# First layer from its second block on: two steps' first products, then two steps' second products

## The chip, the cores and the metric

The kernel runs on one core of one Trainium2 chip. The metric is the device time of one execution in microseconds (us); lower is better. The engines are named as in the profile: PE is the matrix engine, with PEld for its weight loads and PEq for its sequencer; DVE is the vector engine, ACT the scalar engine, POOL the GpSimd engine, and SP the engine that issues nearly all DMAs (its queue is SPq).

## What is computed

```python
x = attn_out.transpose(0, 2, 1, 3).reshape(B * S, H * D)    # 3072 tokens x 320
# attn_out: a gated recurrent attention (mLSTM) over q, k, v, i_gate, f_gate, o_gate
# B, H, S, D = 4, 8, 768, 40

# first layer: w_in 320 x 2048, w_out 2048 x 320
h = x @ w_in
x = (h - np.tanh(h)) @ w_out

# second layer: weights of the same shapes
h = x @ w_in
g = np.where(h >= 1, h, np.where(h <= -1, 0.0, (h + 1) ** 2 / 4))
out = g @ w_out
```

## The kernel before

The 3072 tokens are cut into six blocks of four chunks of 128 tokens (512 tokens to a block). The attention is done in 24 jobs, one for each chunk, in the form of matrix products: t_s holds the scores, d the decay factors (a scan over a broadcast row fb, L460) and then scores times decays (L493), t_n the numerators, t_x the transposed result, t_c the state. A block of the first layer needs the attention of its four chunks.

Each layer works on a block in 16 **steps**, one for each 128 of the 2048 hidden columns. Step f of a block has two parts on PE. The **first products** (`step`, L650) fill one PSUM bank h with 128 hidden columns x 512 tokens: eight matmuls of 512 columns, because x and the weights are each split in a high and a low part. The **second products** (`second`, L702) multiply the result with w_out and add into four banks a, one for each chunk: twelve matmuls of 320 columns. Between the two, in the first layer, four instructions run in a chain: tanh on ACT (L668), h minus tanh on DVE (L669, in the bank itself), the high part gh on ACT (L681), and the low part gl on DVE (L682). When gl is written, the bank h is free again. The second products of a step are issued two steps after its first products (`LAG = 2`). There are two banks for h, and three buffers each of gh and gl (`LAG + 1`).

The second layer has the same shape, but its steps go in groups of four (`GS`): four half-height matmuls that serve all four steps (`rows64`, L629), then the 28 other first products of the four steps, then 48 second products of four earlier steps. Its four h banks are the two of the first layer and two that the attention used.

The order is not written out by hand. Each instruction is given to a planner (`Plan`) with an engine, an estimated duration and a priority; the planner runs through time and gives each engine, among the operations that can start within 150 ns of the first, the one with the lowest priority number. What comes out is a fixed order for each engine. The priority of step i (counted through all blocks and both layers) is about i; that of its elementwise work is i - 3.5 and i - 3; that of the second products issued with it is i + 0.5. The priorities of the attention jobs of block k + 1 are spread over the 16 steps of block k, so attention runs between the steps of the first layer's blocks 0 to 4; in its last block there is none. In the same stretch DVE and ACT also convert the weights (64-bit to 32-bit, L320 to L333), and those of the second layer are stored and loaded again.

Of the kernel before, what the change touches and what calls it, by code (L numbers as in the profile page):

```python
# [56 lines left out]
GS = 4  # L57
# [18 lines left out]
class Plan:  # L76
# [20 lines left out]
    def op(self, eng, ns, prio, fn, r=(), w=(), out=None, lock=False):  # L97
        o = Op()
        o.eng, o.ns, o.prio, o.fn, o.seq, o.out = eng, ns, prio, fn, len(self.ops), out
        o.allocs, o.preds, o.succs = [], set(), []  # L100
        o.bufs, o.fill, o.lock = [], 0, lock
        key = lambda x: x if isinstance(x, tuple) else (x, None)

        for x in map(key, r):
            if x in self.last:
                o.preds.add(self.last[x])
            self.read.setdefault(x, []).append(o)
        for x in map(key, w):
            if x in self.last:
                o.preds.add(self.last[x])  # L110
            o.preds.update(self.read.pop(x, ()))
            self.last[x] = o
        o.preds.discard(o)
        for b in {key(x)[0] for x in (*r, *w)}:
            if isinstance(b, Buf):
                b.users.append(o)
                o.bufs.append(b)
        if any(b.place[0].startswith("late_") for b in o.bufs):
            o.preds.add(self.gate)
        self.ops.append(o)  # L120
        return o
# [110 lines left out]
def mlstm_moe_moe(ctx: ExitStack, tc: tile.TileContext, ig, fg, qk, qk3, q3, nat, w1, w2, cst, out):  # L232
# [63 lines left out]
    def load64(layer, f, prio):  # L296

        if layer == 0 and f in RAW:
            t = wbuf(RAW[f], [128, 8 * WC], U8, "w64")
        else:  # L300
            t = abuf("w64", [128, 8 * WC], U8, 2)
        raw_w[layer, f] = t
        load(prio, lambda: t[:, 0:8 * WC - 3], lambda: (w1, w2)[layer][f].bitcast(U8)[:, 3:8 * WC],
             704, w=[t], rows=5629)
# [23 lines left out]
    def split_w(layer, f, prio):  # L328
        u, a = w32.pop((layer, f))
        w = wt[layer, f] = wbuf(f, [128, 2 * WC], F32R, f"w{f}")  # L330
        op("ACT", act(WC), prio, lambda: nc.scalar.copy(w[:, 0:WC], a()), [u], [(w, 0)])

        vec(prio, WC, lambda e: e.tensor_tensor(  # L333
            out=w[:, WC:2 * WC], in0=a(), in1=w[:, 0:WC].bitcast(F32), op=ALU.subtract), [u, (w, 0)], [(w, 1)])
# [283 lines left out]
    def rows64(k, f, prio):  # L618

        n = BLK[k] * L  # L620
        x, y = x1[1, k], xd[k]
        for j in range(GS):
            hb[f + j] = bank(HTAGS[j], "h")

        def go():
            for j in range(GS):
                r = slice(j % 2 * 64, j % 2 * 64 + 64)
                a = x[r, 4, :n] if j % 2 == 0 else y[r, :n]
                nc.tensor.matmul(hb_[j][:, :n], wt[1, f + j][r, WC + 256:WC + 384], a, start=True, stop=False)  # L629

        hb_ = [hb[f + j] for j in range(GS)]
        op("PE", 200 + GS // 2 * pe(n), prio, go, [*((wt[1, f + j], 1) for j in range(GS)), *xkeys(1, k, 2), y], hb_)

    def step(layer, k, f, prio):
        n = BLK[k] * L
        p = None if layer else bank("h", "h")
        if wide(layer, k, f):
            w, x = wf[f], xf[0]
            for i in range(3):
                op("PE", 2 * pe(n, 128, 2), prio, lambda i=i: nc.tensor.matmul(  # L640
                    p[:, :n], w[:, i * 128:(i + 1) * 128].bitcast(F32), x[:, i, :n], start=(i == 0), stop=(i == 2)),
                   [w, *((x, m) for m in range(BLK[0]))], [p])
            return activate(layer, n, p, prio, True)
        w, x = wt[layer, f], x1[layer, k]
        seq = [(0, 0), (128, 1), (0, 2), (128, 3), (256, 4), (WC, 0), (WC + 128, 1), (WC + 256, 4)]
        if layer:
            p = hb.pop(f)
            seq.pop()
        for i, (c, s) in enumerate(seq):
            op("PE", pe(n), prio, lambda i=i, c=c, s=s: nc.tensor.matmul(  # L650
                p[:, :n], w[:, c:c + 128], x[:, s, :n], start=(i == 0 and not layer), stop=(i == len(seq) - 1)),
               [(w, int(c >= WC)), *xkeys(layer, k, s // 2)], [p])
        return activate(layer, n, p, prio, False)
# [32 lines left out]
    def second(layer, k, f, g, prio):  # L686
        n = BLK[k] * L
        w = wf[f] if wide(layer, k, f) else wt[layer, f]
        gh, gl = g
        first, last = f == 0, f == NF - 1  # L690
        if first:
            acc[k] = [bank(f"a{i}", "a") for i in range(BLK[k])]
        for s in range(BLK[k]):
            A = acc[k][s]
            r = slice(s * L, (s + 1) * L)
            if gl is None:
                seq = [(gh, 384, None)]
            else:
                seq = [(gh, 384, 0), (gh, 384 + WC, 1), (gl, 384, 0)]
            for i, (a, c, key) in enumerate(seq):  # L700
                dt = F32R if gl is not None else F32
                op("PE", pe(DM) if gl is not None else 2 * pe(DM, 128, 2), prio, lambda A=A, r=r, a=a, c=c, i=i, dt=dt: nc.tensor.matmul(  # L702
                    A[:, 0:DM], a[:, r], w[:, c:c + DM].bitcast(dt), start=first and i == 0, stop=last and i == len(seq) - 1),
                   [(w, key), a], [A])
# [65 lines left out]
    def background(f, prio):  # L770
        conv64(1, f, prio)
        u, a = w32.pop((1, f))
        load(prio + 0.5, lambda: w2_d[f], a, 352, [u], [("w2_d", f)], rows=2816)

    def reload(f, prio):
        t = lbuf("w2", [128, WC], F32, 5)
        load(prio, lambda: t.t, lambda: w2_d[f], 352, [("w2_d", f)], [t], rows=2816)
        w32[1, f] = t, lambda: t.t
# [28 lines left out]
    def jobs(k):  # L807
        for i, (a, _) in enumerate(GROUPS):
            if i and a * B == BLK0[k]:
                gates(i, GATES[i])  # L810
                decays(i, DECAYS[i])
        for n in range(BLK0[k], BLK0[k] + BLK[k]):
            if k == 0:
                job(n, lambda s: JOB0 + JOBD * n + JOBS * s, LOAD[n])
            else:
                st = NF * (k - 1) + NF * (n - BLK0[k]) / BLK[k] - AHEAD
                job(n, lambda s: st + s, st - LOADS)
# [12 lines left out]
    for i, (layer, k, f) in enumerate(steps):  # L830
        if layer == 0 and f == 0 and 0 < k < NB - 1:
            jobs(k + 1)
        if i == NF:
            for h in range(NF):
                load64(1, h, NF + 4 * h - 8)
                background(h, NF + 1 + 4 * h)
        if i == n1 - NF:

            def turn():
                att.close()  # L840
                late["p"] = ctx.enter_context(tc.tile_pool(name="late", bufs=1, reuse_waits="tile"))
            P.gate = op("X", 0, i, turn)
            P.gate.preds.update(o for o in P.ops if any(b.place[0] in att_tags for b in o.bufs))
            for h in range(NF):
                reload(h, i + max(0, h - 2))
            for h in range(NF):
                split_w(1, h, i + h + LAG + 1)
            layer2_x(0, i)
        if layer == 1 and f == 0 and k + 1 < NB:
            layer2_x(k + 1, i)  # L850
        u = i - f % GS if layer else i
        if layer and f % GS == 0:
            rows64(k, f, i)
        g[i] = step(layer, k, f, u + 0.01 * (i - u))
        if i == 0:
            P.end_warm = next(o for o in reversed(P.ops) if o.eng == "PE")

            op("PE", 0, i, lambda: None, [], [spare]).preds.add(P.end_warm)
        if i >= LAG:
            p = u + 0.5 + 0.01 * (i - u)  # L860
            second(*steps[i - LAG], g.pop(i - LAG), p)
            if steps[i - LAG][2] == NF - 1:
                evac(*steps[i - LAG][:2], p + 0.005)
# [69 lines left out]
```

## Time and profile before

| what | us |
|---|---|
| median of 3 runs | 816.76 |
| the 3 runs | 816.03 to 818.01 |
| profiled execution | 814.9 |
| its span (first to last instruction) | 813.1 |
| PE busy in the span | 803.5 |

The span is what the trace shows; 1.8 us of the profiled execution lie outside it. The profiled execution is 1.9 us below the median of the runs. The first layer's blocks 1 to 5 lie at about 105 to 475 us of the span, and the second layer behind them. A matmul's row in the trace begins when it is issued and lasts until its modelled end, so rows of neighbouring matmuls overlap; the distance from start to start is what one costs.

### The profile page before, as it was taken

The numbers are of one execution on the slowest core, as the hardware profiler recorded it, in microseconds if no ns is written. First come the engines' busy times: TensorE is split into PE (matmuls) and PEld (weight loads), VectorE is DVE, ScalarE is ACT, GpSimd is POOL, SyncE is SP. The second block draws the span as 40 slices with busy tenths as digits, with TensorE's granted clock in tenths as the row PEclk, the third lists the DMA queues.
The fourth block names the chain that finished last, engine by engine and source line by source line (L and its number), as shares of the span: only waits on it lengthen the run. The fifth ranks groups of instructions, "written<-read, shape, count | busy, mean of one in ns | idle before, by whom it ended". The sixth has DMA issues, their size and how long they took to land.

```text
span 813.1 us, 15218 instructions
## 1 busy us (share of the span) xinstructions
PE 803.5 (99%) x6030; PEld 692.8 (85%) x6034; DVE 570.3 (70%) x922; ACT 429.6 (53%) x810; POOL 147.5 (18%) x147
## 2 busy tenths in 40 slices
PE   9999999999999999999999999999999999999998
PEld 6656888888898888888899888898888889898887
DVE  6899989878888998887456684554646555564644
ACT  4866775675586677544455553443525435342432
POOL 3242122314234335332110200200200201000000
PEclk9999999999999999999999999999999999999999
DMA  8888356686758768771543120100100000000000
GB/s 263 311 261 271 101 194 175 165 260 160 202 164 243 206 188 230 214 178 45 150 116 100 53 72 1 40 33 1 40 33 1 32 1 1 33 1 1 34 1 32
DMA packets 62980, 93.66 MB, mean 115 GB/s; under 512 B 4701, under 2 KB 45501, under 8 KB 62909
## 3 DMA queue, kind: packets, MB, share of 16 engines
q1 hardware_dynamic: 62860, 92.66, 39.2%
q8 instruction: 47, 0.77, 0.4%
q14 instruction: 25, 0.20, 0.1%
q10 hardware_dynamic: 48, 0.03, 0.0%
HBM read 78.88 MB, written 13.80 MB: 114 GB/s over the span
## 4 chain that ended last, share of the span: by engine, by line
PE 90%; DMA 3%; DVE 2%; issue 1%; ACT 1%; SPq 1%; POOL 0%; POOLq 0%; ACTq 0%
PE a L702 40%; PE h L650 37%; PE h L640 3%; PE t_n L529 2%; PE h L629 2%; PE t_n L520 1%; PE t_s L473 1%; PE t_c L558 1%; PE t_s L489 1%; DMA nat<-in_nat_dram 1%; PE t_x L551 1%; DMA w_d<-w 1%; SPq L286 1%; DMA gb<-gr_d 1%; DMA fr_d<-fr 0%
## 5 line engine op out<-in xcount | busy, mean ns | idle before, releaser
L650 PE MATMUL h<-x,w 128*128 128x512 f32 x1376 | 350.1, 397 | 0.1
L702 PE MATMUL a<-w,gh 128*128 128x320 f32 x1472 | 329.3, 310 | 0.0
L650 PEld LDWEIGHTS h<-x,w 128*128 128x128 f32 x1376 | 249.5, 188 | 52.2 <-issue 6.8
L702 PEld LDWEIGHTS a<-w,gh 128*128 128x128 f32 x1472 | 250.0, 188 | 11.0 <-ACT ob L725 1.8
L702 PE MATMUL a<-w,gl 128*128 128x320 f32 x736 | 227.5, 310 | 0.0
L673 DVE TENSOR_SCALAR g<-h 128x512 f32<-128x512 f32 x96 | 63.7, 684 | 114.1 <-PE h L650 114.1
L675 ACT ACTIVATE g<-g,half 128x512 f32<-128x512 f32 x96 | 67.0, 721 | 135.5 <-DVE g L673 135.0
L702 PEld LDWEIGHTS a<-w,gl 128*128 128x128 f32 x736 | 138.2, 188 | 0.3
L669 DVE TENSOR_TENSOR h<-h,g 128x512 f32<-128x512 f32 x88 | 61.2, 695 | 44.0 <-ACT g L668 43.9
L677 DVE TENSOR_TENSOR g<-h,g 128x512 f32<-128x512 f32 x96 | 64.7, 692 | 27.1 <-ACT g L675 26.1
L681 ACT CAST gh<-g 128x512 fp32r<-128x512 f32 x96 | 59.5, 622 | 44.3 <-DVE g L677 43.6
L668 ACT ACTIVATE g<-h 128x512 f32<-128x512 f32 x88 | 52.5, 597 | 53.4 <-PE h L650 52.8
L766 POOL TENSOR_TENSOR x<-xl,x 128x512 fp32r<-128x512 f32 x18 | 25.0, 1420 | 278.1 <-ACT x L757 278.1
L681 ACT CAST gh<-h 128x512 fp32r<-128x512 f32 x88 | 51.4, 585 | 45.3 <-DVE h L669 45.0
L682 DVE TENSOR_TENSOR gl<-h,gh 128x512 fp32r<-128x512 f32 x88 | 60.1, 683 | 19.1 <-ACT gh L681 17.3
L682 DVE TENSOR_TENSOR gl<-g,gh 128x512 fp32r<-128x512 f32 x96 | 62.1, 687 | 4.0 <-ACT gh L681 1.2
L460 DVE TENSOR_TENSOR_SCAN d<-fb,scan_id 128x512 f32<-128x512 f32 x40 | 54.6, 1376 | 1.9 <-DMA fb<-fr_d 1.8
L486 POOL TENSOR_TENSOR xf<-qkraw,xf 120x1024 fp32r<-120x1024 f32 x12 | 32.6, 2713 | 38.1 <-ACT xf L484 34.4
L484 ACT ACTIVATE xf<-qkraw,cs 120x512 fp32r<-120x512 f32 x48 | 32.5, 716 | 6.1 <-PE t_s L489 6.0
L493 DVE TENSOR_TENSOR d<-t_s,d 128x512 f32<-128x512 f32 x48 | 32.0, 681 | 4.4 <-PE t_s L489 2.9
L539 POOL TENSOR_TENSOR nat<-nat,dn 128x320 f32<-128x320 f32 x24 | 21.0, 874 | 70.3 <-DVE dn L538 70.3
L500 POOL TENSOR_TENSOR nat<-nat,isT 128x328 f32<-128x328 f32 x24 | 22.6, 952 | 57.9 <-DMA nat<-in_nat_dram 37.2
(103 smaller groups left out, 765.2 us busy)
## 6 DMA issues: line engine op xcount, KB each, us to landing
w<-in_w_dram SPq DMA_DIRECT2D x32, 703.6 KB
nat<-in_nat_dram SPq DMA_DIRECT2D x24, 484.0 KB
qkraw<-in_qk_dram SPq DMA_DIRECT2D x24, 480.0 KB
fb<-fr_d SPq DMA_DIRECT2D x40, 256.0 KB
w_d<-w SPq DMA_DIRECT2D x16, 352.0 KB
w<-w_d SPq DMA_DIRECT2D x16, 352.0 KB
qkraw<-in_qk_dram SPq DMA_DIRECT2D x24, 160.0 KB
xr_d<-xo SPq DMA_DIRECT2D x24, 160.0 KB
```

The source lines that it names most:

```text
L460: op("DVE", dve(1024), p, lambda o=dk[u][0], i=f[u][0]: nc.vector.tensor_tensor_scan(out=o(), data0=i(), data1=scan_id, initial=0.0, op0=A ...
L484: op("ACT", act(512, 1), at(u - 1), lambda raw=raw, t=t, z=z, cols=cols: nc.scalar.activation(t[:, cols], raw[:, cols], AF.Copy, scale=cs[ ...
L486: vec(at(u - 1), 1024, lambda e, raw=raw, t=t: e.tensor_tensor(out=t.t, in0=raw.t, in1=t.t.bitcast(F32), op=ALU.subtract), [raw, t], [t], ...
L650: op("PE", pe(n), prio, lambda i=i, c=c, s=s: nc.tensor.matmul(p[:, :n], w[:, c:c + 128], x[:, s, :n], start=(i == 0 and not layer), stop= ...
L668: op("ACT", act(n), prio + 0.5 - FFN, lambda: nc.scalar.activation(t[:, :n], p[:, :n], AF.Tanh), [p], [t])
L669: op("DVE", dve(n), prio + 0.5 - FFN, lambda: nc.vector.tensor_tensor(out=p[:, :n], in0=p[:, :n], in1=t[:, :n], op=ALU.subtract), [p, t], [p])
L673: op("DVE", dve(n), prio + 0.5 - FFN, lambda: nc.vector.tensor_scalar(t[:, :n], p[:, :n], -1.0, 1.0, op0=ALU.max, op1=ALU.min), [p], [t])
L675: op("ACT", act(n, 1), prio + 0.5 - FFN, lambda: nc.scalar.activation(t[:, :n], t[:, :n], AF.Square, bias=half[:, 0:1], scale=0.5), [t, "h ...
L677: op("DVE", dve(n), prio + 0.5 - FFN, lambda: nc.vector.tensor_tensor(out=t[:, :n], in0=p[:, :n], in1=t[:, :n], op=ALU.max), [p, t], [t])
L681: op("ACT", act(n), prio + 1 - FFN, lambda: nc.scalar.copy(gh[:, :n], y[:, :n]), [y], [gh])
L682: op("DVE", dve(n), prio + 1 - FFN, lambda: nc.vector.tensor_tensor(out=gl[:, :n], in0=y[:, :n], in1=gh[:, :n].bitcast(F32), op=ALU.subtra ...
L702: op("PE", pe(DM) if gl is not None else 2 * pe(DM, 128, 2), prio, lambda A=A, r=r, a=a, c=c, i=i, dt=dt: nc.tensor.matmul(A[:, 0:DM], a[: ...
```

## The change

The priority of a step in the first layer was its number i. From the second block on (k > 0) it is now that of the even step of its pair, plus 0.01 for the odd one; the same goes for its second products and for its elementwise work. The planner does the rest, for all engines.

```diff
@@ -848,7 +848,7 @@
             layer2_x(0, i)
         if layer == 1 and f == 0 and k + 1 < NB:
             layer2_x(k + 1, i)
-        u = i - f % GS if layer else i
+        u = i - f % (GS if layer else 2 if k > 0 else 1)
         if layer and f % GS == 0:
             rows64(k, f, i)
         g[i] = step(layer, k, f, u + 0.01 * (i - u))
```

The instructions are the same ones in the same number. What follows is the order on three places; the numbers behind w_ tell the weight tiles of the steps apart.

First, PE in the last block of the first layer, where no attention runs. Before, from the first products of step 8 (w_752) to those of step 9 (w_916):

```order
L650 MATMUL h<-x_4521,w_752 128x512 x8
L702 MATMUL a<-w_1853,gh 128x320 x2
L702 MATMUL a<-w_1853,gl 128x320
L702 MATMUL a<-w_1853,gh 128x320 x2
L702 MATMUL a<-w_1853,gl 128x320
L702 MATMUL a<-w_1853,gh 128x320 x2
L702 MATMUL a<-w_1853,gl 128x320
L702 MATMUL a<-w_1853,gh 128x320 x2
L702 MATMUL a<-w_1853,gl 128x320
L650 MATMUL h<-x_4521,w_916 128x512 x8
```

Of the change, from the same first products on:

```order
L650 MATMUL h<-x_4523,w_752 128x512 x8
L650 MATMUL h<-x_4523,w_916 128x512 x8
L702 MATMUL a<-w_1849,gh 128x320 x2
L702 MATMUL a<-w_1849,gl 128x320
L702 MATMUL a<-w_1849,gh 128x320 x2
L702 MATMUL a<-w_1849,gl 128x320
L702 MATMUL a<-w_1849,gh 128x320 x2
L702 MATMUL a<-w_1849,gl 128x320
L702 MATMUL a<-w_1849,gh 128x320 x2
L702 MATMUL a<-w_1849,gl 128x320
L702 MATMUL a<-w_1874,gh 128x320 x2
```

The two steps' first products now stand together, and so do two steps' second products. Over the whole program PE goes from second products straight to first products (a row L702, then a row L650) 87 times before and 40 times now.

Second, the second block, around its step 7 (weight tile w_1897 before, w_1874 in the change, whose low part L333 is made just then; fb, C, x, d and t_s belong to the attention). DVE before, from gl of step 6 to gl of step 7:

```order
L682 TENSOR_TENSOR gl<-h,gh 128x512
L602 TENSOR_TENSOR x_1700<-t_x,x_1700 128x2x128
L606 TENSOR_TENSOR x_1700<-t_x,x_1700 64x128
L357 COPY carry<-mg 32x1
L669 TENSOR_TENSOR h<-h,g 128x512
L493 TENSOR_TENSOR d<-t_s,d 128x512
L682 TENSOR_TENSOR gl<-h,gh 128x512
```

DVE of the change, from gl of step 6 to gl of step 7:

```order
L682 TENSOR_TENSOR gl<-h,gh 128x512
L324 SCALAR_TENSOR_TENSOR w_1306<-w_1251,w_1306 128x704
L333 TENSOR_TENSOR w_1874<-wf,w_1874 128x704
L575 SCALAR_TENSOR_TENSOR C<-C,gb,t_c 80x82
L602 TENSOR_TENSOR x_1698<-t_x,x_1698 128x2x128
L606 TENSOR_TENSOR x_1698<-t_x,x_1698 64x128
L460 SCALAR_TENSOR_TENSOR d<-fb,scan_id 128x512
L669 TENSOR_TENSOR h<-h,g 128x512
L493 TENSOR_TENSOR d<-t_s,d 128x512
L682 TENSOR_TENSOR gl<-h,gh 128x512
```

PE of the change at that place, from the low-part products of step 7 to the first products of step 9 (w_916), which use the same bank:

```order
L650 MATMUL h<-x_806,w_752 128x512 x2
L650 MATMUL h<-x_806,w_1874 128x512 x3
L650 MATMUL h<-x_806,w_752 128x512
L473 MATMUL t_s<-qkraw 128x128 x8
L650 MATMUL h<-x_806,w_752 128x512 x5
L520 MATMUL t_n<-C,q_1762 128x123 x2
L520 MATMUL t_n<-C,q_1762 128x82
L650 MATMUL h<-x_806,w_916 128x512 x7
```

Three more long DVE instructions stand ahead of step 7's chain, and between the end of step 7's first products and those of step 9 there are now no second products.

Third, PE where the second layer begins (L629 is `rows64`; w_1213 and w_1266 are the first layer's last two steps). Before, from the first rows64 on:

```order
L629 MATMUL h<-x_5167,w_5292 128x512
L629 MATMUL h<-xd,w_5325 128x512
L629 MATMUL h<-x_5167,w_5358 128x512
L629 MATMUL h<-xd,w_5391 128x512
L650 MATMUL h<-x_5167,w_5292 128x512 x7
L650 MATMUL h<-x_5167,w_5325 128x512 x7
L650 MATMUL h<-x_5167,w_5358 128x512 x7
L650 MATMUL h<-x_5167,w_5391 128x512 x7
L702 MATMUL a<-w_1266,gh 128x320 x2
L702 MATMUL a<-w_1266,gl 128x320
```

Of the change, from one row ahead of the first rows64 on:

```order
L702 MATMUL a<-w_1213,gh 128x320
L629 MATMUL h<-x_5184,w_5310 128x512
L629 MATMUL h<-xd,w_5324 128x512
L629 MATMUL h<-x_5184,w_5376 128x512
L629 MATMUL h<-xd,w_5390 128x512
L650 MATMUL h<-x_5184,w_5310 128x512 x7
L650 MATMUL h<-x_5184,w_5324 128x512 x7
L650 MATMUL h<-x_5184,w_5376 128x512 x7
L650 MATMUL h<-x_5184,w_5390 128x512 x7
L702 MATMUL a<-w_1213,gh 128x320
L702 MATMUL a<-w_1213,gl 128x320
```

Before, the 12 second products of w_1266 were all that stood between the 28 first products and the next rows64; now 11 of w_1213 stand there as well.

## Rows read from the trace of the kernel before

**Rows 1.** The page's first part: busy us (share of the span), instructions.

```profile
PE 803.5 (99%) x6030; PEld 692.8 (85%) x6034; DVE 570.3 (70%) x922; ACT 429.6 (53%) x810; POOL 147.5 (18%) x147
```

**Rows 2.** Busy time by stretch: stretch, its us, then each engine's busy us.

```profile
85.00:480.00 395.00, 392.43 (x3321) 346.76 (x3321) 314.32 (x520) 241.66 (x479) 104.97 (x99) 1.00 0.57 161
...
398.00:462.00 64.00, 64.00 (x357) 57.95 (x356) 37.59 (x53) 33.23 (x55) 3.79 (x3) 1.00 0.43 121
```

**Rows 3.** The chain that ended last: start, us, what; one step of the last block.

```profile
441.21 1.84 PE h L650 x8
443.05 1.75 PE a L702 x12
```

**Rows 4.** PE in order of time: one matmul, then 15 inside a long run.

```profile
441.05 0.39 PE L650 MATMUL h<-x,w 128*128 128x512 f32 x1
...
608.79 3.56 PE L650 MATMUL h<-x,w 128*128 128x512 f32 x15
```

**Rows 5.** In order of time, one step's chain in the last block.

```profile
442.88 0.45 PE L702 MATMUL a<-w,gh 128*128 128x320 f32 x2
...
443.42 0.60 ACT L668 ACTIVATE g<-h 128x512 f32<-128x512 f32 x1 [1.24 <-PE h L650]
...
445.40 0.69 DVE L682 TENSOR_TENSOR gl<-h,gh 128x512 fp32r<-128x512 f32 x1 [0.66 <-ACT gh L681]
```

**Rows 6.** In order of time on PE: waits in the first layer, in brackets.

```profile
144.94 0.52 PE L551 MATMUL t_x<-cs,x 128*128 128x128 f32 x3 [0.38 <-DVE x L546]
...
185.42 0.76 PE L520 MATMUL t_n<-C,q 120*128 120x123 f32 x5 [0.68 <-POOL q L510]
...
331.78 0.21 PE L370 MATMUL t_i<-cs,ig 32*128 32x32 f32 x1 [0.77 <-DVE x L606]
```

**Rows 7.** In order of time, DVE and PE where the second layer begins.

```profile
464.46 0.50 PE L629 MATMUL h<-x,w 64*128 64x512 f32 x1
...
465.12 6.66 PE L650 MATMUL h<-x,w 128*128 128x512 f32 x28
...
473.05 1.35 DVE L677 TENSOR_TENSOR g<-h,g 128x512 f32<-128x512 f32 x2 [0.19 <-ACT g L675]
...
473.47 0.50 PE L629 MATMUL h<-x,w 64*128 64x512 f32 x1
...
474.88 2.11 PE L650 MATMUL h<-x,w 128*128 128x512 f32 x8
```

**Rows 8.** DVE in order of time in the second block.

```profile
132.47 0.42 DVE L602 TENSOR_TENSOR x<-t_x,x 128x256 fp32r<-128x256 f32 x1
132.91 0.28 DVE L606 TENSOR_TENSOR x<-t_x,x 64x128 fp32r<-64x128 f32 x1
133.22 1.23 DVE L460 TENSOR_TENSOR_SCAN d<-fb,scan_id 128x512 f32<-128x512 f32 x1
134.36 0.67 DVE L669 TENSOR_TENSOR h<-h,g 128x512 f32<-128x512 f32 x1
134.95 0.69 DVE L493 TENSOR_TENSOR d<-t_s,d 128x512 f32<-128x512 f32 x1
...
137.29 0.85 DVE L333 TENSOR_TENSOR w<-wf,w 128x704 fp32r<-128x704 f32 x1
138.07 0.87 DVE L322 TENSOR_TENSOR w<-w,cvb 128x704 int32<-128x704 f32 x1
```

**Rows 9.** POOL in order of time in the second block.

```profile
142.42 0.75 POOL L510 TENSOR_TENSOR q<-q,gb 120x256 f32<-120x256 f32 x1 [2.87 <-PE a L702]
...
143.53 0.73 POOL L539 TENSOR_TENSOR nat<-nat,dn 128x320 f32<-128x320 f32 x1
```

**Rows 10.** SP's queue and DVE: broadcasts issued, and the scan that waited.

```profile
175.20 1.29 SPq L286 DMA_DIRECT2D fb<-fr_d  x2
...
182.91 1.22 DVE L460 TENSOR_TENSOR_SCAN d<-fb,scan_id 128x512 f32<-128x512 f32 x1 [1.22 <-DMA fb<-fr_d]
```

**Rows 11.** PE in order of time: t_s of a job.

```profile
133.76 1.16 PE L473 MATMUL t_s<-qkraw 40*128 40x128 f32 x16
```

## The prediction

> **What bounds the kernel now.** I read the page's busy times first. PE is busy for 99% of the span, DVE for 70%, ACT for 53% [rows 1]. So PE sets the end, and the change can act in two ways only: through what PE's instructions cost in another order, and through the moments at which PE stands still. The instructions are the same, so nothing else can be saved.
>
> How much standing still is there? The busy time by stretch gives 392.43 us of PE in the 395 us from 85 to 480, in which the changed steps lie: 2.57 us idle, and none in the 64 us of the last block, where no attention runs [rows 2]. A wait is longer than its idle time by the modelled end of the matmul ahead of it, some 0.15 us (the last matmul's 0.39 us against the 0.23 us that one costs), so all waits together are some 4 us. The order of time on PE shows the longest: a t_x that waits for x, a t_n that waits for q, a t_i that waits until the t_x before it is read [rows 6]. All three are attention work; none is a wait of the steps' own chain. One more lies at the start of the second layer, below.
>
> Is the chain of a step tight? In the last block the second products behind a step's first ones begin at 442.88, tanh at 443.42, and gl is written at 446.09 [rows 5]: 3.2 us from the end of the first products to a free bank. A step's first products take 1.84 us and its second ones 1.75 [rows 3].
>
> **The turns from second to first products.** Inside a long run a matmul of 512 columns costs (3.56 - 0.39) / 14 = 0.226 us [rows 4], so eight should cost 1.81. In the last block, where a step begins behind second products and PE never waits, they cost 1.84 [rows 3]. A turn thus costs some 0.025 us (the rows are rounded to 0.01, so 0.02 to 0.035). By the order, 47 of 87 such turns go: 47 x 0.025 = 1.2 us; I take **-1.1 us**, since some of the joined runs are cut again by attention work, and 0.5 to 1.6 as bounds.
>
> The Trainium skill, "TensorE: Matmul & The Clock Gate", section "Back-to-back issue gap", gives the distance of warm back-to-back matmuls as a function of their columns alone, with weights loaded ahead beside running matmuls; by that page this term would be nothing. Its figure for 512 columns, 216 ns, is below the 226 ns of the run here, and the 230 ns behind a turn differ from both, so this trace speaks against it.
>
> **The bank and the buffers.** With pairs, the first products of step i + 2 need the bank of step i. For an even step there lie between: the odd step's first products and two steps' second ones, 1.84 + 3.5 = 5.3 us; for an odd step: two steps' second products and the even step's first, the same 5.3. Before it was second, first, second: also 5.3. Against 3.2 this leaves 2.1 us on either order. One thing is new: there are three gh buffers, so gh of an odd step must wait until the second products of the step three earlier are done, and these now come right behind its first products, 1.75 us later. But tanh and the subtraction take that long anyway: 0.54 us from the end of the first products to tanh (443.42 - 442.88), 0.6 for it, and 0.67 for the DVE instruction [rows 8], 1.8 in all. In the last block I therefore expect no wait, and **0** for this edit; DVE and ACT hide it with 59% and 52% of that stretch busy [rows 2]. If that cover were gone, a late bank would cost PE its lateness, once a pair.
>
> **Where DVE is full.** In blocks 1 to 4 attention instructions stand between a step's chain, and the 2.1 us can go. The tightest place that I found in the new order is the one shown, in the second block around its step 7. Count from the end of step 6's first products. Its gl is there at 3.2. Behind it on DVE stand two weight instructions (0.78 each, from start to start, of the 704-wide kind), three attention ones (0.44 and 0.31 by their starts; the third, of 82 columns, at most as the 128-wide one, 0.28), a scan (1.14), then step 7's subtraction (0.59), an attention product (0.69) and gl (0.69) [rows 8]: bank free at 3.2 + 1.56 + 1.03 + 1.14 + 1.97 = 8.9. PE has until then 24 second products (24 x 0.146 = 3.5), 16 first ones (16 x 0.23 = 3.7), t_s (1.16) [rows 11] and t_n (0.76 for a part of it that waited) [rows 6]: 9.1. So it is just in time, with nothing left for a late operand. Before, no weight instruction and no scan stood between. Taking busy times instead of starts (0.07 more for each of seven) DVE is late by some 0.3; a scan whose broadcast is late, as one was by 1.22 us [rows 10], hands that on. I take **+0.2**, with bounds 0 and 1.2.
>
> **The attention waits.** The t_x wait (144.94): x was late because POOL did the two products with q ahead of the product with dn, from 142.42 to 143.53 [rows 9]. In the new order POOL does the product with dn first. I take **-0.4** of its 0.38 idle and some 0.15 behind the modelled end. The t_i wait (331.78): it needs the bank that the t_x before it leaves. Before, 12 second and 3 first products stood between (2.45 us); now 11 first and 4 second ones (3.1 us), 0.65 more against 0.77 idle: **-0.4**, as DVE's reading may come later too. The t_n wait (185.42) comes from a group's broadcasts: they were issued at 175.20 and reached the scan at 182.91, 7.7 us later [rows 10]. The t_n stands later on PE now, but in the new order two scans of that group stand on DVE ahead of a step's chain, so I leave it, **0**: what t_n no longer waits, the bank does. For places not read I add **+0.4**: attention work is put at a moment that the planner holds for right, and I see no reason why a new arrangement should have no new waits; bounds 0 and 2.5, the idle of today once more.
>
> **The start of the second layer.** rows64 and what follows normally take 0.66 us (464.46 to 465.12); the second time it is 1.41 (473.47 to 474.88) [rows 7], a wait of 0.75, because the four banks are free only when DVE has done with the four steps before, at 474.40. The new order puts 11 more second products in between, 11 x 0.146 = 1.6 us. DVE has no more to do before that than it had. So the wait goes: **-0.75**, 0 as the other bound if DVE is later by as much.
>
> **Sum.** -1.1 + 0.2 - 0.4 - 0.4 + 0.4 - 0.75 = -2.05, about -2.1 us. The profiled execution of 814.9 would become 812.8; it stood 1.9 below the median of the runs, so against that median the time is 816.8 - 2.1 = **814.7 us**. Differences below 0.3%, 2.4 us here, are about what a measurement of this kernel cannot tell from no change; the forecast stays just inside.
>
> **Rivals.**
> - *The waits only move.* The turns are saved, and each wait that goes comes back elsewhere: -1.1, **815.7 us**. For it: the planner's durations are the same, and the waits of today are all of the attention. Against: the 0.75 us of the second layer have nothing to do with that.
> - *Most waits go.* A pair's second products lie together, so attention has longer stretches to be late in. The first layer's waits go down from 4 us to 1.4, and with the turns and the second layer that is -1.1 - 2.6 - 0.75, **812.3 us**. For it: two of the three long ones have a reason that the order removes. Against: at the place in the second block there is no slack.
> - *Slower: banks late where DVE is full.* Chains come two at a time, and where a scan (1.14) and a weight instruction or two stand between a subtraction and its gl, the bank is late. It decides from 2.1 us of extra DVE work in a chain on. DVE is busy for 314 of 395 us [rows 2], so per pair of steps (7.2 us and attention) there is often that much. At 0.5 us each in 12 of the 32 pairs of blocks 1 to 4 that is +6, with the turns and the second layer +4.2: **821 us**. Against: in the one place worked out it is only just late. The same page's section "Architectural detail" calls ACT and DVE strict first-in first-out queues, which the order of time here agrees with, and which would make such a wait hold up what stands behind it.
> - *Turns cost nothing*, as the columns alone would have it: the sum without its first term, -1.0, **815.8 us**; rows 3 and 4 speak against it.
> - *The change does nothing* is out: the order has changed on every engine.
>
> **How the numbers follow.** The forecast 0.38, waits that move 0.22, most waits gone 0.22, slower 0.13, turns for nothing 0.05. Of the forecast somewhat under half lies beyond 2.4 us of gain (0.16). Faster by over 0.3%: 0.16 + 0.22 + 0.02 = 0.40. Within: 0.22 + 0.20 + 0.05 = 0.47. Slower: 0.13. The range runs from 811.9, just past the case in which most waits go, to 818.3: the worse bounds for the turns (-0.5) and the place in the second block (+1.2), a third of the unread 2.5 (+0.8), and nothing for t_x, t_i and the second layer, +1.5 in all; the slower rival beyond it is left out.
>
> **What would show it.** PE in the last block: runs of 16 first products in 1.81 + 1.84 = 3.65 us or a little less, followed by 24 second ones, with no idle. At the second rows64 the distance to the first products back at 0.66. PE's idle from 85 to 480 at about 2 us; no wait for x at the t_x of the job in the second block, and perhaps a wait for gl (L682) at its step 9. The prediction is wrong if PE waits for gl at many steps, or if the idle stretches stay as long while the runs get no shorter.

## The result and the profile after

| | median us | runs | range |
|---|---|---|---|
| kernel before | 815.41 | 15 | 812.29 to 818.95 |
| changed kernel | 821.23 | 15 | 816.33 to 873.13 |

The ratio of the changed kernel to the one before is 1.0064, with a 95% interval of 1.0038 to 1.009: **slower**, by more than the 0.3% that can be told from no change, and beyond the range of the prediction. The first of the 15 runs (873.13 us) had a granted clock of 0.851 from end to end and is left out of the ratio; it was also the profiled one. So the profile after is that of the same kernel run once more (experiment e1: 820.33 us, ratio 1.0048; profiled execution 819.1, span 817.3).

Its page and its busy time by stretch (stretch, us, busy us of PE, PEld, DVE, ACT and POOL, granted clock, DMA share, GB/s), which answer to [rows 1, 2]:

```profile
PE 804.5 (98%) x6034; PEld 694.3 (85%) x6034; DVE 568.2 (70%) x922; ACT 431.9 (53%) x812; POOL 144.8 (18%) x147
85.00:480.00 395.00, 388.54 (x3289) 343.68 (x3289) 307.47 (x513) 241.33 (x477) 101.37 (x97) 0.99 0.56 161
398.00:462.00 64.00, 64.00 (x361) 58.26 (x361) 36.80 (x54) 32.66 (x55) 3.87 (x3) 1.00 0.45 127
```

PE now stands still for 6.46 us of the 395 us, against 2.57 before, and the mean clock of that stretch is 0.99 instead of 1.00. The last block has no idle time, as before. So the loss lies where attention runs. The profile's list of what PE waited for (us in total, times, longest), without what lies ahead of the stretch:

```profile
PE t_x L551 <- DVE x L546: 2.8, 2, 2.4
PE t_n L520 <- DVE d L493: 1.8, 1, 1.8
...
PE h L650 <- DVE gl L682: 0.8, 1, 0.8
PE t_i L370 <- DVE x L606: 0.6, 1, 0.6
PE h L650 <- DVE w L333: 0.3, 1, 0.3
```

Two waits stick out: 2.4 and 1.8 us. The first one in order of time, SP's queue, ACT, then DVE, then PE:

```profile
132.80 0.41 SPq L286 DMA_DIRECT2D qkraw<-in_qk_dram  x1
...
138.01 0.19 ACT L463 COPY wc<-d 128x4 f32<-128x4 f32 x1
141.18 0.72 ACT L484 ACTIVATE xf<-qkraw,cs 120x512 fp32r<-120x512 f32 x1 [2.98 <-DMA qkraw<-in_qk_dram]
141.81 0.57 ACT L681 CAST gh<-h 128x512 fp32r<-128x512 f32 x1
...
142.90 0.77 ACT L331 CAST w<-wf 128x704 fp32r<-128x704 f32 x1
...
138.15 0.70 DVE L669 TENSOR_TENSOR h<-h,g 128x512 f32<-128x512 f32 x1 [0.57 <-ACT g L668]
...
142.41 0.69 DVE L682 TENSOR_TENSOR gl<-h,gh 128x512 fp32r<-128x512 f32 x1 [2.73 <-ACT gh L681]
143.01 0.48 DVE L546 TENSOR_TENSOR x<-t_n,nat 128x320 f32<-128x320 f32 x1
143.70 2.84 DVE L333 TENSOR_TENSOR w<-wf,w 128x704 fp32r<-128x704 f32 x1 [0.20 <-ACT w L331]
...
143.64 0.52 PE L551 MATMUL t_x<-cs,x 128*128 128x128 f32 x3 [2.42 <-DVE x L546]
143.92 2.37 PE L650 MATMUL h<-x,w 128*128 128x512 f32 x5
146.59 1.35 PE L650 MATMUL h<-x,w 128*128 128x512 f32 x3 [0.30 <-DVE w L333]
```

Read it from PE upwards. The t_x waits for x (L546); x stands on DVE behind gl (L682), which waits for gh; and gh, a step's cast, stands on ACT behind an instruction of another job, the split of its q and k (L484), which waits 2.98 us for its transfer. The cast's own operand, h from L669, was written at 138.85, and yet the cast began only at 141.81, behind the split. A wait for data that nobody on PE needed yet has stopped a step's chain, because ACT took its instructions in order here. In the kernel before, ACT came to that split only after the gh cast, state work and a weight conversion, at 144.04, and did not wait:

```profile
141.33 0.58 ACT L681 CAST gh<-h 128x512 fp32r<-128x512 f32 x1
...
144.04 0.72 ACT L484 ACTIVATE xf<-qkraw,cs 120x512 fp32r<-120x512 f32 x1
```

The first row shows the issue of that transfer at 132.80, 8.4 us before ACT could start. With nothing else under way the planner counts 4.1 us for it (1.4 us ahead, 1.77 by its formula for 480 KB, 0.9 behind), and so it put the split where its data seemed to be there.

The second place is of the same kind, with nat in the place of qkraw: ACT, DVE and PE in order of time, and the issue of nat on SP's queue:

```profile
242.33 0.60 ACT L668 ACTIVATE g<-h 128x512 f32<-128x512 f32 x1
245.36 1.28 ACT L504 ACT_TABLE_LOAD   x1 [2.43 <-DMA nat<-in_nat_dram]
...
247.03 0.57 ACT L681 CAST gh<-h 128x512 fp32r<-128x512 f32 x1
...
247.63 0.69 DVE L682 TENSOR_TENSOR gl<-h,gh 128x512 fp32r<-128x512 f32 x1 [2.29 <-ACT gh L681]
248.24 0.68 DVE L493 TENSOR_TENSOR d<-t_s,d 128x512 f32<-128x512 f32 x1
...
248.98 0.90 PE L520 MATMUL t_n<-C,q 120*128 120x123 f32 x6 [1.82 <-DVE d L493]
...
238.76 0.45 SPq L286 DMA_DIRECT2D nat<-in_nat_dram  x1
```

This load was issued behind three others at 236.13 to 238.66, and ACT could start 6.6 us after its issue. What held gh up here was not the wait of 2.43 us alone: a table load of 1.28 us and the sigmoid of nat stood behind the wait and ahead of the cast.

Behind both stops PE runs slowly for a while. The busy time in pieces of 2 us, columns as above:

```profile
140.00:142.00 2.00, 1.22 (x9) 0.93 (x7) 0.00 (x0) 0.82 (x2) 0.35 (x1) 1.00 0.15 35
142.00:144.00 2.00, 0.36 (x4) 0.39 (x4) 1.39 (x3) 2.00 (x4) 2.00 (x4) 1.00 0.00 0
144.00:146.00 2.00, 2.00 (x7) 1.28 (x5) 2.00 (x1) 0.61 (x3) 1.79 (x1) 0.51 0.69 223
146.00:148.00 2.00, 1.70 (x6) 1.24 (x6) 2.00 (x4) 1.29 (x3) 0.00 (x0) 0.64 0.56 138
...
248.00:250.00 2.00, 1.02 (x7) 1.00 (x8) 2.00 (x3) 2.00 (x5) 0.00 (x0) 0.96 0.12 35
250.00:252.00 2.00, 2.00 (x8) 1.69 (x7) 1.40 (x3) 1.15 (x2) 0.00 (x0) 0.50 0.49 139
252.00:254.00 2.00, 2.00 (x56) 1.29 (x58) 1.68 (x3) 1.42 (x3) 0.21 (x1) 0.68 0.99 247
```

After PE had waited for 2.42 and 1.82 us, the granted clock fell to about 0.5, the 1.2 GHz level, and came back some 3 us later. Busy time at half the clock counts as busy in the page, so the idle sum does not show this part: the five pieces from 144 and from 248 on lose (0.49 + 0.36 + 0.04 + 0.50 + 0.32) x 2 = 3.4 us of full-clock time.

**The account.** PE's first product of the second block starts at 113.54 in the profile before and at 111.76 after; in the runs of this study it lies anywhere from 111 to 116, whatever the order behind it, so I count from there on. Before, 813.1 - 113.5 = 699.6 us of the span follow; after, 817.3 - 111.8 = 705.5: **+5.9**. Of that +3.9 is more idle time, +3.4 the clock, and -1.2 the turns by the prediction's estimate; the sum is +6.1.

That is one execution, with a fall of the clock at both places. The mean granted clock of every execution tells how much of the loss needs such a fall. Five of e1's 12 had 1.000, and took 819.2 us on the mean; of the 35 of the kernel before that ran beside them 21 had 1.000, and took 815.0. So 4.2 us are lost with no fall of the clock at all. The seven of e1 with 0.998 or less took 821.2; the kernel before has ten such executions too, and they took 818.0.

### The profile page after: what moved, and what is told of

Its sections match the earlier page's. It is cut to its first block, busy times and chain, and to the rows that moved or that the text cites. A ratio compares the mean times of both kernels' runs of the same rounds, so it can differ in the third digit from the quotient of the medians.

```text
span 871.3 us, 15295 instructions
## 1 busy us (share of the span) xinstructions
PE 865.0 (99%) x6034; PEld 728.0 (84%) x6034; DVE 571.0 (66%) x922; ACT 433.7 (50%) x812; POOL 148.1 (17%) x147
## 4 chain that ended last, share of the span: by engine, by line
PE 99%; DVE 0%; ACT 0%; issue 0%; POOL 0%; POOLq 0%
PE a L702 42%; PE h L650 40%; PE h L640 3%; PE t_n L529 2%; PE h L629 2%; PE t_s L473 2%; PE t_n L520 2%; PE t_c L558 2%; PE spare L796 1%; PE t_s L489 1%; PE t_x L551 1%; PE t_f L451 1%; DVE w L333 0%; ACT xf L484 0%; PE t_i L370 0%
## 5 line engine op out<-in xcount | busy, mean ns | idle before, releaser
L650 PE MATMUL h<-x,w 128*128 128x512 f32 x1376 | 372.5, 422 | 1.4 <-DVE w L333 1.4
L702 PE MATMUL a<-w,gh 128*128 128x320 f32 x1472 | 350.5, 324 | 0.0
L650 PEld LDWEIGHTS h<-x,w 128*128 128x128 f32 x1376 | 257.3, 193 | 76.2 <-issue 7.1
L702 PEld LDWEIGHTS a<-w,gh 128*128 128x128 f32 x1472 | 258.7, 192 | 10.0 <-issue 1.9
L702 PE MATMUL a<-w,gl 128*128 128x320 f32 x736 | 237.9, 323 | 0.0
L673 DVE TENSOR_SCALAR g<-h 128x512 f32<-128x512 f32 x96 | 65.9, 686 | 141.4 <-PE h L650 141.4
L675 ACT ACTIVATE g<-g,half 128x512 f32<-128x512 f32 x96 | 69.5, 724 | 157.5 <-DVE g L673 157.0
L702 PEld LDWEIGHTS a<-w,gl 128*128 128x128 f32 x736 | 141.1, 192 | 0.3
L669 DVE TENSOR_TENSOR h<-h,g 128x512 f32<-128x512 f32 x88 | 61.1, 695 | 43.5 <-ACT g L668 43.5
L682 DVE TENSOR_TENSOR gl<-h,gh 128x512 fp32r<-128x512 f32 x88 | 60.1, 685 | 25.4 <-ACT gh L681 23.4
L682 DVE TENSOR_TENSOR gl<-g,gh 128x512 fp32r<-128x512 f32 x96 | 61.9, 686 | 2.9
L484 ACT ACTIVATE xf<-qkraw,cs 120x512 fp32r<-120x512 f32 x48 | 32.6, 717 | 19.3 <-PE t_s L489 15.2
L486 POOL TENSOR_TENSOR xf<-qkraw,xf 120x1024 fp32r<-120x1024 f32 x12 | 29.4, 2449 | 40.1 <-ACT xf L484 19.3
L320 ACT ACTIVATE cvb<-w,half 128x704 bf16<-128x704 int8 x32 | 30.0, 937 | 6.2 <-DVE w L322 3.2
```

The costliest lines, as they stand in the source:

```text
L484: op("ACT", act(512, 1), at(u - 1), lambda raw=raw, t=t, z=z, cols=cols: nc.scalar.activation(t[:, cols], raw[:, cols], AF.Copy, scale=cs[ ...
L669: op("DVE", dve(n), prio + 0.5 - FFN, lambda: nc.vector.tensor_tensor(out=p[:, :n], in0=p[:, :n], in1=t[:, :n], op=ALU.subtract), [p, t], [p])
L673: op("DVE", dve(n), prio + 0.5 - FFN, lambda: nc.vector.tensor_scalar(t[:, :n], p[:, :n], -1.0, 1.0, op0=ALU.max, op1=ALU.min), [p], [t])
L675: op("ACT", act(n, 1), prio + 0.5 - FFN, lambda: nc.scalar.activation(t[:, :n], t[:, :n], AF.Square, bias=half[:, 0:1], scale=0.5), [t, "h ...
L682: op("DVE", dve(n), prio + 1 - FFN, lambda: nc.vector.tensor_tensor(out=gl[:, :n], in0=y[:, :n], in1=gh[:, :n].bitcast(F32), op=ALU.subtra ...
```

## The experiments

Each expectation was written before its run. In the first four the theories are: A, one place makes the loss; B, it is spread; C, the clock by itself.

**Where is the loss? e1 to e4.** The changed kernel again, and the pairs in some blocks only (k counts from 0, so k == 1 is the second block):

```diff
-        u = i - f % (GS if layer else 2 if k > 0 else 1)
+        u = i - f % (GS if layer else 2 if k > 1 else 1)         # e2
+        u = i - f % (GS if layer else 2 if k == 1 else 1)        # e3
+        u = i - f % (GS if layer else 2 if k == NB - 1 else 1)   # e4
```

e1, unchanged: 

> The changed kernel itself, once more, for a profile at the full granted clock. The record has it 5 us slower than before, and its one profile at a granted clock of 0.85 shows a wait of 1.5 us in the second block (first products wait for the low weight part of step 7, L333). Theory A (one place): PE waits 1 to 3 us more than before in the second block, 110 to 175 us, and in the rest of the first layer no more than before. Theory B (spread): the added waits lie in all of blocks 1 to 4, each well below 1 us. Theory C (clock): PE's waits are no longer than before; the executions with a mean granted clock below 1.0 are the slow ones, and those at 1.0 are equal to before.

e2, from the third block on: 

> Pairs from the third block on, the second block in single steps as before. Theory A: the loss is gone, -1 to -2 us against before. Theory B: three quarters of the loss stay, +3 to +4 us. Theory C: the loss goes with the clock, between +2 and +4 us, and the profile shows no added waits.

e3, the second block alone: 

> Pairs in the second block only. Theory A: all of the loss, +4 to +6 us. Theory B: a quarter of it, about +1 us. Theory C: about +1 us, by the clock.

e4, the last block alone: 

> Pairs in the last block of the first layer only, where no attention runs. Eight turns fewer save 0.2 us, and the wait of 0.75 us at the second rows64 goes: -1 us by theories A and B, within what can be told from no change. Theory C: if longer runs of first products lower the clock by themselves, the mean granted clock is below 1.0 here too.

| | median us | ratio to before (815.83) | 95% interval |
|---|---|---|---|
| e1 | 820.33 | 1.0048 | 1.0025 to 1.007 |
| e2 | 812.30 | 0.9959 | 0.9939 to 0.9978 |
| e3 | 819.07 | 1.0027 | 1.0005 to 1.005 |
| e4 | 814.84 | 0.9979 | 0.9964 to 0.9994 |

Pairs make the kernel faster where the second block keeps its single steps (e2), and slower with the second block alone (e3). Neither theory had the sizes: e2 gains 3.5 us by the medians where A expected 1 to 2, and e3 loses 3.2 where A expected 4 to 6 and B 1. e4 is as expected. In e3 the same ACT split waits for the same transfer (2.54 us); PE's waits there are

```profile
145.83 0.52 PE L551 MATMUL t_x<-cs,x 128*128 128x128 f32 x3 [1.67 <-DVE x L546]
149.04 0.96 PE L650 MATMUL h<-x,w 128*128 128x512 f32 x3 [1.54 <-DVE w L333]
```

and the clock stayed at 1.00 all through: 3.2 us lost with no part of the clock. The second of these waits has a cause that I had not named: the weights' low part (L333) took 3.10 us there, beside a POOL instruction, and 0.85 to 0.89 in that profile's seven other rows of the kind (`w<-wf`; more at the end). So C does not carry the loss, which the executions at a clock of 1.000 say as well. The second block is the first place, as A had it; but e1's second stop lies in the third block, where e2 has the same pairs and no such wait. It isn't pairs in a block as such, but what order the planner happened to make with them.

**Is it ACT's place in the order? e5, e6.** From here on theory A is ACT's queue (a transfer that lands later than the planner thinks, with a step's cast behind it), and B the prediction's slower rival (banks late because DVE is full). The pairs stay; only the planner's notion of when two kinds of loads land is moved. Nothing on the chip is touched but the order that follows; but that is a new order on every engine from there on, not for ACT alone.

```diff
-                o.end = dma + self.DMA_OUT
+                o.end = dma + self.DMA_OUT + self.LATE.get(o, 0.0)
...
-                load(ld, ..., 480, w=[qs[u]])                     # qkraw
+                load(ld, ..., 480, w=[qs[u]], late=4000.0 if n == STACK else 0.0)   # e5
+                load(ld, ..., 480, w=[qs[u]], late=4000.0)                           # e6
...
-        load(ld, ..., w=[(nt, 0), (nt, 1), (nt, 2)], rows=3872)   # nat
+        load(ld, ..., rows=3872, late=4000.0 if n >= STACK else 0.0)                 # e6
```

e5: 

> The changed kernel, but the planner is told that the qkraw loads of the first stacked job (the one whose split on ACT stood 2.98 us for its data at 138 to 141 us) land 4 us later than it assumes; nothing else is altered, and the order moves only from there on. Theory A (in pairs the planner puts ACT's L484 split ahead of a step's gh cast, ACT's in-order queue stands for the transfer, and the gl, x and t_x behind it come late; PE stops and its granted clock then falls): the t_x wait of 2.4 us near 143.6 and the stretch of clock 0.5 to 0.64 behind it (some 1.7 us) go, the second such place near 246 us (t_n 1.8 us and its clock) stays: 820.5 less 2 to 4 us, 816.5 to 818.5. Theory B (the pairs make banks late because DVE is full, wherever ACT stands): 820 to 821, the wait comes back as h <- DVE w L333 or gl L682.

e6: 

> As the kernel with one late job, but the planner counts 4 us more for the qkraw and the nat loads of all stacked jobs, so that L504 too is planned behind the casts that it held up at 243 to 245 us. Theory A: both stops of PE go, 813 to 816, at or below the kernel before (815.6). Theory B: 819 to 821. If it stays above 817.5 with both ACT waits gone, something else in the second and third blocks holds the loss.

Measured beside a kernel before of 814.98: e5 815.97, ratio 1.0006 (0.9991 to 1.002); e6 811.54, ratio 0.996 (0.9945 to 0.9975). One number for one job's loads takes away nearly all of the loss, and both numbers turn it into a gain; both are below what theory A expected (816.5 to 818.5, and 813 to 816). In e5 the split now stands behind the gh casts that ACT does at 140.77, 144.79 and 147.22, and waits for nothing; its line in order of time on ACT, and behind it e6's busy time by stretch:

```profile
148.96 1.35 ACT L486 ACTIVATE xf<-qkraw,cs 120x512 fp32r<-120x512 f32 x2
```

```profile
85.00:480.00 395.00, 392.80 (x3333) 349.67 (x3332) 311.47 (x520) 239.16 (x481) 107.97 (x99) 1.00 0.58 164
```

(L486 is the former L484, two lines down.) In e6 PE's idle time is 2.20 us with pairs everywhere and DVE as busy as before, and PE waits for no gl: B is out as the main cause. (In e1 one bank was late in that way, by 0.76 us at 192.03.) e5's profile does not have the stop near 246 that I expected to stay. It has a t_s at 189.01 (1.76 us), which waits for an instruction of DVE that took 3.50 us beside POOL's and 1.22 at other places (L488), and a t_x at 261.25 (1.88 us) with a fall of the clock behind it; at neither does ACT wait for a qkraw or nat load.

**Does the number help any order? e7, e8.** The same number in the kernel before, and in e2: 

> The kernel before (single steps) with the same planner number as the run with qkraw and nat late: a control. PE waited for no late transfer there, so theory A expects no change, 815.6 within 1 us. If it is faster by 2 us or more, the number helps any order and what it gives in pairs is not told by the pairs.

> Pairs from the third block on (812.3 before) with the same planner number. Theory A: that kernel's second block is in the order of before and had no stop of over 1 us, so little to win: 811 to 813. Theory B: the same; the run is for a version that beats both kernels.

Beside the same kernel before as e5 and e6: e7 813.12, ratio 0.9973 (0.9957 to 0.9989); e8 812.89, ratio 0.9971 (0.9956 to 0.9986). Theory A expected no change from e7 and got 1.9 us, just under the 2 us that I had set as the sign of a help for any order. So of the 0.9% that the number gives the pairs (1.0048 to 0.996), some 0.3% is had by single steps too, and I have not traced from where: e7's profiled execution, with a span of 817.6, was its slowest and says nothing of the median. With the number in both, pairs against single steps are 811.54 to 813.12, 0.2% faster by the medians, and their intervals overlap. e8 gains nothing over e2, as expected.

**The other way round: e11.** Single steps, and the planner told that the first such load lands 2 us sooner (`late=-2000.0 if n == STACK else 0.0` in the kernel before): 

> The opposite on the kernel before: single steps, but the planner counts 2 us less for the qkraw loads of the first stacked job, which puts ACT's first L484 split ahead of a gh cast and a t_n step there, as the pairs did. Theory A: ACT stands for the transfer at 138 to 143 us, PE stops for 2 us or more with a fall of the granted clock behind it, and the kernel is 2 to 6 us slower than before without any pairs. Theory B (the pairs themselves make the loss): no change, 0.998 to 1.002.

Measured: 822.4 us beside 815.25, ratio **1.0088** (1.0064 to 1.0112), more than the 2 to 6 us that theory A expected and at least the loss of the pairs (1.0064 and 1.0048), without one pair. ACT and PE in order of time, then the clock behind it:

```profile
136.44 0.47 ACT L506 ACTIVATE nat<-nat 128x320 f32<-128x320 f32 x1 [2.21 <-DMA nat<-in_nat_dram]
140.43 0.72 ACT L486 ACTIVATE xf<-qkraw,cs 120x512 fp32r<-120x512 f32 x1 [3.52 <-DMA qkraw<-in_qk_dram]
...
141.94 1.61 PE L652 MATMUL h<-x,w 128*128 128x512 f32 x5 [3.27 <-ACT w L333]
...
142.00:144.00 2.00, 2.00 (x8) 1.74 (x9) 2.00 (x3) 1.93 (x8) 2.00 (x3) 0.75 0.01 2
144.00:146.00 2.00, 2.00 (x9) 2.00 (x8) 2.00 (x4) 0.98 (x3) 0.36 (x1) 0.50 0.44 129
```

The same split stands for the same transfer (issued at 133.55), PE stops and the clock falls. What stands behind the split and stops PE is here a weight's cast (L333) and not a gh. Nor is this stop all of the loss: PE's idle time from 85 to 480 is 10.22 us in this profile. A second long stop came at a place at which the number did not aim, and there ACT stood for a third transfer, a store of weights:

```profile
292.35 0.94 ACT L322 ACTIVATE w<-w,half 128x704 f32<-128x704 int8 x1 [3.42 <-DMA w_d<-w]
...
297.90 0.52 PE L553 MATMUL t_x<-cs,x 128*128 128x128 f32 x3 [2.44 <-DVE x L548]
```

(x stands on DVE behind a gl, which waits for a gh that ACT did at 296.05, behind this instruction.) The mechanism needs no pairs, and no particular load; the pairs made the planner choose an order with it.

**Do the two places add up? e10.** The number for nat alone: 

> The changed kernel with the planner's 4 us more for the nat loads of the stacked jobs alone: the second place (L504 at 243 to 245 us, t_n 1.8 us and the clock behind it) should go and the first stay. Theory A, if the two places add up: half of what both numbers gave (1.0048 to 0.996), about 1.000 to 1.002. If it is 1.004 or more, the second place held little and the rest of the gain with both numbers came from elsewhere in the order.

817.03 us, ratio 1.0026 (1.0004 to 1.0047): between the two bounds that I gave, and a quarter of the way from 1.0048 to 0.996 where theory A expected about half. One number each took off 0.42% (e5) and 0.22%, and both 0.88%; with intervals of some 0.2% on each this neither shows nor excludes that the two places add up. Its profile has the first stop still (t_x 1.33 us, then 1.69 for w L335, at 146 to 150) and none near 246.

**What does the clock cost? e9.** The matmuls just ahead of the first stop, a t_c product, are done eleven times instead of once, into the same place:

```diff
-                    start=True, stop=True), [K, V], [pc])
+                    start=True, stop=True) for _ in range(11 if n == 9 and k == 2 else 1)], [K, V], [pc])
```

> The changed kernel with the last t_c product of one job (the matmuls that PE runs just before it stops at 141.2 us) repeated 10 times more into the same place, with no other order moved: some 2 us of idle matmuls fill most of the stop of 2.4 us; the stop itself (ACT's wait for qkraw) stays. If the fall of the granted clock behind the stop (0.51 and 0.64 in 144 to 148) comes from PE's standing still and costs time of its own, the clock stays at 1.00 there and the run is 1.3 to 1.8 us under the changed kernel, ratio to before about 1.003 instead of 1.005. If the clock falls all the same, or its fall costs nothing (theory: only the wait counts), the time is that of the changed kernel, 1.005, or above it by what the repeats add.

820.67 us, ratio 1.0054 (1.0032 to 1.0077): no gain. PE and DVE in order of time, and the clock behind the filled stop:

```profile
145.72 1.95 PE L558 MATMUL t_c<-nat 128*120 128x123 f32 x24
147.51 0.49 PE L551 MATMUL t_x<-cs,x 128*128 128x128 f32 x3
147.76 1.41 PE L650 MATMUL h<-x,w 128*128 128x512 f32 x5
150.56 0.96 PE L650 MATMUL h<-x,w 128*128 128x512 f32 x3 [1.39 <-DVE w L333]
...
147.18 3.33 DVE L333 TENSOR_TENSOR w<-wf,w 128x704 fp32r<-128x704 f32 x1 [0.20 <-ACT w L331]
...
148.00:150.00 2.00, 1.17 (x6) 0.60 (x4) 2.00 (x1) 0.28 (x2) 1.76 (x1) 1.00 0.61 192
```

In this profile the clock stayed at 1.00, also at the second place, where nothing was filled (so whether it would have fallen in that execution without the fill can't be told), and the median did not move. Behind the filled stop lies a wait of 1.39 us for the weights' low part (L333), as in e3 and e10 without any fill (1.54 and 1.69): ACT's stop had delayed it, and then it took 3.33 us beside POOL. So at the first place the slow clock was mostly hidden: in e1 the five products at half speed end 0.3 us before L333 lets the next ones go, and the 0.30 us wait behind them would have been longer at full speed. What stays to the clock there is the next three products, 1.18 us from start to start (146.59 to 147.77) against 0.7 at full clock: 0.5 us, not the 1.3 to 1.8 that I expected. At the second place no such wait lies behind it (the next ones in brackets come after 256), and there its 1.7 us count in that execution. This fill was tried at the first place alone.

**A cruder mending: e12.** Every transfer counted 3 us later (`DMA_OUT` 3900 instead of 900): 

> Pairs with every transfer counted 3 us later by the planner (3900 ns instead of 900 behind each), not only qkraw and nat: a cruder mending of the same model. Theory A: both ACT stops go, 0.995 to 0.999; but steps that were planned early enough before may now be planned too late (weights, fb), which can give 2 to 4 us back, 1.000 to 1.003.

814.55 us, ratio 0.9995 (0.998 to 1.0011), between my two cases: the loss of the pairs is gone, and with it their gain.

## Why the prediction was wrong, step by step

- **The turns** (-1.1). Right. In the last block 16 first products now take 3.65 us from start to start where two runs of eight took 3.68 [rows 3], as said:

```profile
460.60 3.81 PE L650 MATMUL h<-x,w 128*128 128x512 f32 x16
464.25 0.45 PE L702 MATMUL a<-w,gh 128*128 128x320 f32 x2
...
478.63 0.50 PE L629 MATMUL h<-x,w 64*128 64x512 f32 x1
...
479.30 0.97 PE L650 MATMUL h<-x,w 128*128 128x512 f32 x3
```

- **The second rows64** (-0.75). Right: 0.67 us to the first products instead of 1.41 [rows 7]. e4, which has little more than this and the last block's turns, came out at -0.2% with an interval of -0.36 to -0.06%, 0.5 to 2.9 us; the terms give 0.75 + 8 x 0.025 = 0.95.
- **The bank in the last block** (0). Right, no idle there.
- **The second block around step 7** (+0.2). No bank was late there: step 7's gl was written at 156.48, and PE came to the bank at 156.87.
- **The t_i wait** (-0.4). Gone as said. **The t_n wait** (0). As said, in kind: the t_n of 185 no longer waits, and a bank does at 192.03 (gl, 0.76 us), behind two scans that DVE began at 186.06 after 1.29 us for their broadcast; a t_i waits before it (0.56).
- **The t_x wait** (-0.4). **This step failed.** The wait did not go but grew, from 0.38 to 2.42 us. POOL did change its order as read, but x was then late for a reason that I had not looked at: gl stood ahead of it on DVE, gh ahead of that, and on ACT a transfer ahead of gh. I had followed what POOL and DVE do at that place and not what ACT does, and I had taken the landing of loads as given.
- **Places not read** (+0.4, bounds 0 to 2.5). **This is the term that was mis-sized.** I took the idle time of the kernel before as its bound, which is no bound: it is what one order happened to leave. Two stops of 2.4 and 1.8 us came, others moved, +3.9 us of idle time in all, and behind the two stops the clock, which stood in no term, for another 3.4 us as the rows of that execution count it (of which over 1 us was hidden, as said at e9). Without a fall of the clock the loss was 4.2 us.

The slower rival had the size (821 us) but not the mechanism: operands of t_x and t_n were late and not banks, through ACT's queue and a transfer and not through DVE's work, and in two places and not twelve. The sentence that I set beside it, the Trainium skill, "TensorE: Matmul & The Clock Gate", section "Architectural detail", that ACT and DVE are strict first-in first-out queues, is the rule by which it went; the 2.98 us of ACT's wait with the cast behind it agree with it. I had used it against DVE alone. From the second block on, e6's profile takes 811.6 - 114.4 = 697.2 us, 2.4 less than before, near the -2.05 of my sum without such a stop; one profile each, and e6 has the planner's other number too.

Not settled: what e7 gains, why the planner's order is that sensitive, and how much of the loss at the first place would go if POOL and DVE did not meet there. e2 (812.30, ratio 0.9959) and e6 (0.996) beat both kernels, and I can't tell the two apart.

## What to carry to other kernels

When a planner or a compiler makes the order anew, ask of every instruction that waits for a transfer what now stands behind it on its engine, and compare the transfer's time in the trace, from issue to the reader's start (here 6.6 and 8.4 us), with what the planner counts for it (4.1). The idle time of today's order is no bound for tomorrow's; two stops of some 2 us each undo the gain of 47 turns and one boundary. Where such a change comes out wrong, one planner number moved for the loads at the place helps to tell whether the idea or the order is to blame; try it on the order of before as well, as e7 shows.

## What the runs showed of the hardware

- The granted clock of a kernel whose PE is busy for 98% of the span can still fall to half for about 3 us: behind the stops of 2.42 and 1.82 us in e1 and of 3.27 in e11. The length of the stop did not decide it: behind 1.67 us in e3 and 2.44 in e11 the clock stayed at 1.00, and in e12 it fell (0.62 and 0.53 from 153 to 157) behind two waits of only 0.83 and 0.70 us. The Trainium skill, "TensorE: Matmul & The Clock Gate", "Part 1: The HAM clock gate (the "warmup" mystery)", says that the clock goes by how busy the array has been of late and has two levels; these rows agree, and do not tell which stop brings a fall.
- The low part of a 704-wide weight tile (L333) takes 0.85 us on DVE [rows 8] and took 2.84 (e1), 3.10 (e3), 3.26 (e10) and 3.33 (e9) behind the first stop, beside POOL's own 120x1024 difference; e1's seven other rows of this kind (`w<-wf`) have no POOL instruction beside them and took 0.85 to 0.89:

```profile
143.42 2.37 POOL L486 TENSOR_TENSOR xf<-qkraw,xf 120x1024 fp32r<-120x1024 f32 x1
```

In all four L333 ends some 0.75 us behind that instruction. In the kernel before, where L333 (at 148.33) began 0.1 us ahead of it, L333 took 0.88 us and POOL's instruction 3.04. The Trainium skill, "Trainium Architecture — The Big Picture", "What this means for kernel authors", says that DVE and GpSimd share a port pair under an exclusive lock; the rows fit, and no run here took POOL's instruction away to prove it.
